# Four VectorE steps over 4096 columns, the load of b ahead, and a new order of all steps, in a gated recurrence with a rational feed-forward on one core

## The chip, the cores and the metric

The program runs on one core of one Trainium2 chip. The metric is the device time in microseconds of that core. Before the change the median of three runs is 218.05 us (217.76 to 218.08).

A core has five engines, each with its own queue of instructions that it works off in order: TensorE (matmuls; PE in the profile, its weight loads PEld), VectorE (DVE), ScalarE (ACT), GpSimd (POOL) and SyncE (SP, which here only issues transfers). Engines wait for each other through semaphores. Transfers are issued by an engine and then run by themselves.

## The reference

Two parts, the second fed by the first. The first is a recurrence with a gate per channel over 4 batches, 8 heads, 768 positions and a head size of 48. The second is a feed-forward layer over the 3072 tokens, 384 to 2048 to 384, with a quotient of two polynomials between its two products.

```python
f = 1.0 / (1.0 + np.exp(-f_logit))
for t in range(S):
    state = f[:, :, t, :, None] * state + np.einsum('bhd,bhe->bhde', k[:, :, t], v[:, :, t])
    y[:, :, t] = np.einsum('bhd,bhde->bhe', q[:, :, t], state)
...
h = x @ w_in
h2 = h * h
h3 = h2 * h
P = a[0] + a[1] * h + a[2] * h2 + a[3] * h3
Q = 1.0 + np.abs(b[0]) * np.abs(h) + np.abs(b[1]) * h2
g = P / (Q + 1e-06)
return (g @ w_out).astype(np.float32)
```

## The kernel before, in words

The work is cut into 12 units: a unit is one batch and 256 positions (3 stretches of positions, 4 batches). Within a unit the recurrence is done for two chunks of 128 tokens with matmuls, and the layer then takes the unit's 256 tokens as the columns of 16 blocks of 128 rows of the 2048, so a whole unit of the layer is a tile of 128 x 4096 and a quarter of it (four blocks) is 128 x 1024.

The steps of a unit, by the names that the order uses, with the lines of their functions:

- loads: `ld` of f, k, q on SP's queue and of v on POOL's (L200); the weights `wi` and `wo` in four pieces each on POOL's queue (L206, L212); the small `a` and `b` by `ab_` (L219), on SP's or ACT's queue.
- gate: `ef` and `ls` (ACT, L278 and L283) make log decay; `cs` sums it along positions (PE, L293); `A` takes its exponentials (ACT, L309); `xa` multiplies q and k by them (DVE, L315).
- attention: `T` turns q and k (PE, L327), `Te` takes that out of PSUM (L337 on ACT, L339 on DVE), `sc` multiplies q and k (PE, L352), `mk` masks (DVE, L360), `vm` copies a part of v (POOL, L367), `yb` and `yi` build the output (PE, L374), `kv` and `si` the next state (PE, L421 and L432), `ae` and `st` scale it (ACT L445, DVE L449), `ye` takes the output out of PSUM, scaled, as xT (ACT, L439).
- layer: `h` multiplies by w_in, four blocks to a call (PE, L458); `hy` takes the result out of PSUM as bf16 (ACT, L488); `sq` squares (DVE, L492; `sa` does the same on ACT from PSUM, L496); `ab` clears the sign bits (DVE, L500); the denominator's sum z + h2 is made by `u` on PE (L508), by `zv` on DVE (L518) or by `zd`, an accumulating DMA that POOL issues (L522); `ln` or `lz` (ACT, L513, L526) and `ex` (ACT, L530) make the reciprocal as exp(-log); `p1`, `p2`, `pm` (DVE, L534, L539, L548) and `tv` (DVE, L556) or `ta` (an accumulating DMA from POOL, L552) build the numerator in `gall`; `gm` multiplies by the reciprocal (DVE, L560); `o` multiplies by w_out, four blocks to a call and 128 tokens at a time (PE, L570); `oe` takes that out of PSUM (L577) and `so` stores it (L583).
- `cz`, `cu`, `ci`, `cm` fill constants, `fa`, `fb`, `fr` turn a and b into factors, `dz` issues matmuls whose result nobody reads (L302).

The order is written out by hand: one string, `ORDER`, lists every step, and each engine's queue is the steps of that engine in the order of the string. The numbers behind a step's name are the unit, then the range of blocks or head pairs; `@n` names one of four PSUM slots of 4 KB a partition, each of which is free again when what was in it has been taken out; a last letter names the engine (`s` ACT, `v` DVE, `a` ACT's queue); `>name` holds a load back until the named step is done. The semaphores follow from the tiles: a step waits for whoever wrote what it reads and for whoever still reads what it overwrites. Tiles have few buffers: `hy` and `gall` (the key `g`) three of 128 x 4096, `h2` and `z` two, `lq` and `qi` one, the loaded f, k, q, v three each.

```python
    def p1(n, m0, m1):
        s = unit(n)
        return nc.vector.tensor_scalar(fl(big(s, "g", "gall", 3), m0, m1), fl(s["hy"], m0, m1),
```

In the order before, VectorE's `sq`, `ab`, `pm` and `gm` take a unit in halves (2048 columns) or quarters, while `p1` and `p2` of units 1 to 10 already take 4096.

Of the kernel before, what the change touches and what calls it, by code (L numbers as in the profile page):

```python
# [113 lines left out]
def kernel(  # L114
# [371 lines left out]
    def hy(n, m0, m1):  # L486
        s = unit(n)
        nc.scalar.copy(fl(big(s, "hy", "hy", 3), m0, m1), fl(s["hp", m0], 0, m1 - m0))  # L488
# [140 lines left out]
```

## Time and profile before

| what | value |
|---|---|
| median of 3 runs | 218.05 us (217.76, 218.05, 218.08) |
| span of the profiled execution, first to last instruction | 216.3 us |
| TensorE busy | 203.2 us, 3166 matmuls |
| VectorE busy | 202.7 us, 246 instructions |
| ScalarE busy | 200.8 us, 211 instructions |
| GpSimd busy | 81.6 us, 91 instructions |
| granted TensorE clock | 1.000 |
| moved by DMA | 42.13 MB |

How to read it: the profile is one execution, with a start and a length for every instruction. A row of the timeline has the start in microseconds, the length, the engine, the line of the kernel, the operation, `out<-in` with the shapes, and how many instructions the row merges; in square brackets stands how long the engine was idle before it and who ended that. A row of the groups has the count, then busy time in microseconds and the mean of one in nanoseconds, then idle time before the group's instructions. Lengths overlap: an instruction's row starts a little before the row ahead of it has ended, so the time that one instruction costs in a full queue is the distance from its start to the next start.

### The profile page before, as it was taken

The page shows a single profiled execution, that of the slowest core. Times are in us where ns is not written, and L with a number is a line of the kernel's source. Part 1 is how long each engine was busy: PE and PEld are TensorE (multiplying, and loading weights), DVE is VectorE, ACT ScalarE, POOL GpSimd, SP SyncE. Part 2 cuts the span into 40 slices and gives each one's busy share as a digit, 9 for nine tenths or more (in the row PEclk, how much of TensorE's full clock was granted, in tenths as well). Part 3 has the DMA queues.
Part 4 walks back from the last instruction along what each step waited for, and adds up shares of the span by engine and source line. Part 5 has one row for each costly group of instructions (what it writes and reads, how often), then busy time and mean ns, then how long its engine had stood idle before and what let it go on. Part 6 is the DMA issues. An engine that isn't in the chain of part 4 may idle for free.

```text
span 216.3 us, 7159 instructions
## 1 busy us (share of the span) xinstructions
PE 203.2 (94%) x3166; PEld 140.1 (65%) x3166; DVE 202.7 (94%) x246; ACT 200.8 (93%) x211; POOL 81.6 (38%) x91
## 2 busy tenths in 40 slices
PE   6989989699799999999999999999999999999993
PEld 2457658468377657658758658668668678676551
DVE  3588999999999999999999999999999999999991
ACT  4746899999999999999999999999999999999991
POOL 5250247120157803014954205954232516433300
PEclk9999999999999999999999999999999999999999
DMA  5999999999598999958999997999889793999863
GB/s 132 248 226 194 243 212 226 207 221 250 136 246 143 231 237 271 149 101 195 197 232 216 211 251 179 173 234 222 160 159 228 142 162 70 170 194 188 154 234 145
DMA packets 60910, 42.13 MB, mean 195 GB/s; under 512 B 51152, under 2 KB 54992, under 8 KB 60880
## 3 DMA queue, kind: packets, MB, share of 16 engines
q0 software_dynamic: 21232, 22.81, 66.0%
q1 hardware_dynamic: 39360, 18.68, 33.7%
q8 instruction: 24, 0.39, 0.7%
q10 hardware_dynamic: 288, 0.20, 0.3%
q14 instruction: 6, 0.05, 0.1%
HBM read 25.17 MB, written 4.72 MB: 138 GB/s over the span
## 4 chain that ended last, share of the span: by engine, by line
ACT 42%; DVE 21%; PE 18%; DMA 8%; issue 6%; POOL 3%; POOLq 0%; ACTq 0%; DVEq 0%
ACT qi L530 11%; ACT hy L488 10%; PE op L570 9%; ACT lq L526 8%; DMA fn<-in_f_logit_dram 4%; DMA z<-h 4%; PE warm L302 3%; DVE gall L548 3%; ACT A L309 3%; DVE scm L360 3%; DVE qkp L315 3%; PE hp L458 2%; DVE gall L560 2%; DVE gall L556 2%; ACT qkT L337 2%
## 5 line engine op out<-in xcount | busy, mean ns | idle before, releaser
L570 PE MATMUL op<-w_out_sb,gall 128*128 128x384 bf16 x384 | 70.1, 326 | 0.4 <-ACT hy L488 0.4
L458 PE MATMUL hp<-xT,w_in_sb 128*128 128x256 bf16 x564 | 65.3, 272 | 1.3 <-ACT xT L439 1.1
L458 PEld LDWEIGHTS <-w_in_sb 128*128 128x128 bf16 x564 | 55.0, 98 | 11.0 <-issue 2.8
L570 PEld LDWEIGHTS <-gall 128*128 128x128 bf16 x384 | 35.5, 98 | 23.6 <-DVE gall L560 0.9
L488 ACT CAST hy<-hp 128x1024 bf16<-128x1024 f32 x48 | 47.4, 1073 | 1.7 <-PE hp L482 1.2
L530 ACT ACTIVATE qi<-lq 128x2048 bf16<-128x2048 f32 (+1 forms) x26 | 46.9, 1845 | 0.0
L367 POOL COPY vmp<-vn 128x128 bf16<-128x128 bf16 x24 | 33.7, 1417 | 32.1 <-DMA vn<-in_v_dram 18.9
L526 ACT ACTIVATE lq<-z 128x2048 f32<-128x2048 bf16 (+1 forms) x20 | 36.9, 1846 | 0.6 <-DMA z<-h 0.5
L552 POOL DMA_DIRECT2D gall<-hy x17 | 14.8, 926 | 50.7 <-ACT A L309 11.5
L522 POOL DMA_DIRECT2D z<-h x18 | 17.3, 1065 | 36.3 <-issue 10.5
L560 DVE TENSOR_TENSOR gall<-gall,qi 128x2048 bf16<-128x2048 bf16 (+1 forms) x26 | 29.6, 1143 | 0.3 <-ACT qi L530 0.2
L548 DVE TENSOR_TENSOR gall<-gall,h 128x2048 bf16<-128x2048 bf16 (+1 forms) x26 | 29.4, 1138 | 0.0
L492 DVE TENSOR_TENSOR h<-hy 128x2048 bf16<-128x2048 bf16 (+1 forms) x26 | 27.3, 1059 | 1.5 <-ACT hy L488 1.4
L360 DVE TENSOR_TENSOR scm<-sc,mask 128x1024 bf16<-128x1024 f32 x24 | 28.4, 1211 | 0.0
L309 ACT ACTIVATE A<-cs 128x768 f32<-128x768 f32 (+1 forms) x26 | 19.6, 816 | 0.0
L500 DVE TENSOR_SCALAR z<-hy 128x2048 uint16<-128x2048 uint16 (+1 forms) x28 | 17.1, 618 | 0.1
L534 DVE TENSOR_SCALAR gall<-hy,a_sb 128x4096 bf16<-128x4096 bf16 (+1 forms) x14 | 16.9, 1210 | 0.2 <-ACT hy L488 0.2
L539 DVE TENSOR_SCALAR hy<-hy,a_sb 128x4096 bf16<-128x4096 bf16 (+1 forms) x14 | 16.6, 1184 | 0.0
L200 POOL DMA_DIRECT2D vn<-in_v_dram x12 | 13.2, 1104 | 2.2 <-PE y L374 2.2
L315 DVE TENSOR_TENSOR qkp<-kn,A 128x768 bf16<-128x768 f32 (+1 forms) x13 | 11.5, 887 | 2.0 <-ACT A L309 2.0
L278 ACT ACTIVATE fn<-fn 128x768 f32<-128x768 f32 (+1 forms) x13 | 10.7, 825 | 2.8 <-DMA fn<-in_f_logit_dram 2.7
L337 ACT COPY qkT<-tp 128x1024 f32<-128x1024 f32 (+1 forms) x12 | 12.5, 1041 | 0.7 <-PE tp L327 0.7
(72 smaller groups left out, 262.2 us busy)
## 6 DMA issues: line engine op xcount, KB each, us to landing
gall<-hy POOLq DMA_DIRECT2D x16, 512.0 KB, 6.7
z<-h POOLq DMA_DIRECT2D x15, 512.0 KB, 7.4
fn<-in_f_logit_dram SPq DMA_DIRECT2D x11, 384.0 KB, 7.4
kn<-in_k_dram SPq DMA_DIRECT2D x11, 384.0 KB, 9.8
qn<-in_q_dram SPq DMA_DIRECT2D x11, 384.0 KB, 7.2
out_dram<-osb SPq DMA_DIRECT2D x11, 384.0 KB, 4.1
vn<-in_v_dram POOLq DMA_DIRECT2D x12, 192.0 KB, 8.0
w_in_sb<-in_moe_w_in_dram POOLq DMA_DIRECT2D x4, 384.0 KB, 8.2
```

What stands on the lines that cost most here:

```text
L309: nc.scalar.activation(t, src, AF.Exp, scale=1.0 if x else -1.0)
L315: return nc.vector.tensor_mul(s["qk"][:, :, x, hh, 0:D], s["qk"[x]][:, hh].rearrange("p h i d -> p i h d"), A_sb[:, :, x].rearrange("p i ( ...
L360: return nc.vector.tensor_mul(t, s["sc", g].rearrange("s r a i t -> s (r a) (i t)"), mb)
L367: nc.gpsimd.tensor_copy(s["vm"][:, :, :, 32 * x:32 * x + 16], src)
L458: nc.tensor.matmul(t[:, m - m0, :], w_in_sb[:, kk, m * P:(m + 1) * P], s["x"][:, kk].rearrange("p i j t -> p (i j t)"), start=(kk == 0), s ...
L488: nc.scalar.copy(fl(big(s, "hy", "hy", 3), m0, m1), fl(s["hp", m0], 0, m1 - m0))
L492: return nc.vector.tensor_mul(fl(big(s, "h2", "h2", 2), m0, m1), fl(s["hy"], m0, m1), fl(s["hy"], m0, m1))
L526: nc.scalar.activation(fl(lq, m0, m1), fl(s["z"], m0, m1), AF.Ln, scale=regs[2], bias=1.0 + 1e-6)
L530: nc.scalar.activation(fl(qi, m0, m1), fl(lq, m0, m1), AF.Exp, scale=-1.0)
L548: return nc.vector.tensor_mul(fl(s["g"], m0, m1), fl(s["g"], m0, m1), fl(s["h2"], m0, m1))
L560: return nc.vector.tensor_mul(fl(s["g"], m0, m1), fl(s["g"], m0, m1), fl(qi, m0, m1))
L570: nc.tensor.matmul(s["op", j][:, j, 0:DM], s["g"][:, m, P * j:P * j + P], w_out_sb[:, m, :], start=(s["on", j] == 1), stop=(s["on", j] == KF))
```

## The change

The order string is written anew: 861 steps become 823. What it does differently, as counts over the whole program:

| step | before | after |
|---|---|---|
| `sq` on DVE | 18 halves, 8 quarters | 9 whole, 2 halves, 8 quarters |
| `sa` on ACT | 4 quarters | none |
| `ab` | 20 halves, 8 quarters | 9 whole, 2 halves, 8 quarters |
| `pm`, `gm`, each | 22 halves, 4 quarters | 9 whole, 4 halves, 4 quarters |
| `tv` on DVE | 6 halves, 3 quarters | 4 halves, 1 quarter |
| `ta` by DMA | 16 halves, 1 quarter | 18 halves, 3 quarters |
| `zv` on DVE | 2 halves | 1 half, 1 quarter |
| `zd` by DMA | 15 halves, 3 quarters | 16 halves, 2 quarters |
| `hy` | 48 on ACT | 47 on ACT, 1 on DVE |
| `ye` | all on ACT | unit 8 and the first piece of unit 0 on DVE |
| `oe` | last unit's first half on DVE | that and unit 10 on DVE |

The whole ones, 4096 columns at once, are those of units 2 to 10. All other steps, the matmuls among them, are the same in number and shape, and stand in another order: `a` is loaded ahead of f on SP's queue; unit 2's f is held back behind `mk 0 1` as before, but `mk 0 1` now comes ahead of `mk 0 0`; the last of the w_in pieces is issued behind unit 1's v and `vm` steps.

The first and the last lines of the string and some between (those that are left out change as well), and the functions:

```diff
 ORDER = """
-ld 0 f 2 4; cz 0; ab_ b a; cu 0; cz 1; ld 0 f 0 2; ld 1 f; ci; cu 1; ld 0 v; ld 0 k 0 2; ld 0 k 2 4; fa
-ld 0 q 2 4; ef 0 2 4; ls 0 2 4; cm; ef 0 0 2; dz 9 @2; cs 0 2 4 @2; fr; cz 3; ls 0 0 2; ld 0 q 0 2; ab_ a s
-ld 1 k; dz 5 @3; cs 0 0 2 @3; ef 1; ld 1 q; ls 1; vm 0 1; A 0 1 0 2; wi 12 16 >ls.1; dz 4 @0; cs 1 @0
-A 0 1 2 4; xa 0 1 0 2; A 0 0 2 4; wi 8 12; cz 2; A 0 0 0 2; xa 0 1 2 4; dz 3 @1; kv 0 @2; wi 4 8
-xa 0 0 0 2; si 0 0; ae 0; dz 1 @1; T 0 0 2 @1; wi 0 4; xa 0 0 2 4; st 0 0; Te 0 0 2 s; T 0 2 4 @3; A 1 1
...
-ex 3 8 16; o 2 1 12 16; st 5 0; zd 4 0 8; o 2 0 12 16; mk 5 1; o 2 0 4 8; ex 3 0 8; p1 4 0 16; yi 5 1 @3
...
-tv 11 8 12; o 11 1 0 4; gm 11 8 12; o 11 0 0 4; ex 11 12 16; tv 11 12 16; o 11 0 8 12; gm 11 12 16
-oe 10 0 2 s; so 10 0 2 s; o 11 1 8 12; o 11 0 12 16; oe 11 0 1 v; so 11 0 1 s; o 11 1 12 16; oe 11 1 2 s
-so 11 1 2 a
+cu 0; ab_ a s; ab_ b a; cz 3; ld 0 f 2 4; ld 0 f 0 2; cz 0; cu 1; dz 9 @0; ld 1 f; cz 1; ld 0 q 2 4; ci; cz 2
+ld 0 k 2 4; cm; ld 0 k 0 2; ld 0 v; ld 0 q 0 2; fa; ld 1 k; ld 1 q; ef 0 0 2; dz 4 @1; ef 0 2 4; fr; ls 0 2 4
+ef 1; cs 0 2 4 @0; ls 0 0 2; A 0 0 2 4; cs 0 0 2 @2; A 0 1 2 4; dz 5 @1; xa 0 0 2 4; A 0 0 0 2; ls 1; vm 0 1
+wi 8 12; xa 0 1 2 4; A 0 1 0 2; wi 12 16 >ls.1; T 0 2 4 @0; xa 0 1 0 2; wi 4 8; Te 0 2 4; kv 0 @3; vm 0 0
+xa 0 0 0 2; sc 0 1 @1; ld 1 v; T 0 0 2 @2; mk 0 1; si 0 0; Te 0 0 2 s; ae 0; ld 2 f >mk.0.1; sc 0 0 @2; st 0 0
...
+ld 3 k; vm 1 0; kv 1 @0; ld 4 f; A 2 1; vm 1 1; ab 0 12 16; ld 3 q; wi 0 4; si 1 0; ae 1; A 2 0; ld 4 q
...
+yb 5 2 4; o 1 0 4 8; ld 8 v; ye 5 s; st 5 1; ld 9 q; T 6 @2; p1 4 0 16; oe 1 0 2 s; cs 7 @0; Te 6 s; so 1 0 2 s
...
+gm 11 12 16; ex 11 0 4; o 11 0 8 12 @3; tv 11 0 4; ex 11 4 8; o 11 0 12 16; gm 11 0 4; o 11 1 12 16; oe 9 0 2 s
+gm 11 4 8; o 11 0 0 4; oe 10 0 2 v; so 9 0 2 s; o 11 0 4 8; o 11 1 0 4; so 10 0 2 s; oe 11 0 1 v; o 11 1 4 8
+so 11 0 1 s; oe 11 1 2 s; so 11 1 2 a
 """
...
     def ye(n, *args):
-        k0, k1 = [x for x in args if x != "s"] or (0, KD)
+        k0, k1 = [x for x in args if x not in ("s", "v")] or (0, KD)
         s = unit(n)
         if "x" not in s:
             s["x"] = at.tile([P, KD, 2, UB, R], BF16, name="xT", bufs=2)
-        return nc.scalar.mul(s["x"][:, k0:k1].rearrange("p k i j t -> p j (k i) t"),
-                             s["y"][:, :, k0 * C:k1 * C].rearrange("p j (k t) -> p j k t", t=R), regs[0])
+        dst = s["x"][:, k0:k1].rearrange("p k i j t -> p j (k i) t")
+        src = s["y"][:, :, k0 * C:k1 * C].rearrange("p j (k t) -> p j k t", t=R)
+        if "v" in args:
+            return nc.vector.tensor_scalar(dst, src, sig[:, 0:1], None, op0=ALU.mult)
+        return nc.scalar.mul(dst, src, regs[0])
...
-    def hy(n, m0, m1):
-        s = unit(n)
-        nc.scalar.copy(fl(big(s, "hy", "hy", 3), m0, m1), fl(s["hp", m0], 0, m1 - m0))
+    def hy(n, m0, m1, eng="s"):
+        s = unit(n)
+        (nc.scalar.copy if eng == "s" else nc.vector.tensor_copy)(
+            fl(big(s, "hy", "hy", 3), m0, m1), fl(s["hp", m0], 0, m1 - m0))
```

143 lines of the change are left out of this document (67 added, 76 removed).

## The prediction

> **What bounds the kernel now.** I read the page first, then the busy time by stage, then the instruction groups by shape, then the timeline of the start and of the end.
>
> ```profile
> PE 203.2 (94%) x3166; PEld 140.1 (65%) x3166; DVE 202.7 (94%) x246; ACT 200.8 (93%) x211; POOL 81.6 (38%) x91
> ...
> 0.00:10.00 10.00, 8.02 (x31) 3.31 (x32) 4.49 (x28) 6.35 (x11) 3.85 (x15) 1.00 0.94 185
> 10.00:20.00 10.00, 9.19 (x206) 6.34 (x204) 8.10 (x14) 4.50 (x9) 3.90 (x6) 1.00 1.24 216
> ...
> 30.00:210.00 180.00, 173.88 (x2730) 122.86 (x2731) 178.95 (x190) 178.93 (x180) 71.65 (x67) 1.00 1.01 195
> ```
>
> The columns are stage, length, then PE, PEld, DVE, ACT, POOL, granted clock, DMA share, GB/s. From 30 to 210 us VectorE is busy 178.95 of 180 and ScalarE 178.93. TensorE shows 173.88, but a matmul's row overlaps the next, so that figure flatters it. No queue is the single bound; VectorE is idle for 1.05 us in those 180, so what it saves or gains there moves the end nearly one to one. Its other idle time, 13.6 less 1.05, lies in the start and in the end:
>
> ```profile
> 190.54 5.40 PE L458 MATMUL hp<-xT,w_in_sb 128*128 128x256 bf16 x48 [0.17 <-ACT xT L439]
> 201.26 11.53 PE L570 MATMUL op<-w_out_sb,gall 128*128 128x384 bf16 x68
> ...
> 210.57 0.69 DVE L560 TENSOR_TENSOR gall<-gall,qi 128x1024 bf16<-128x1024 bf16 x1 [0.15 <-ACT qi L530]
> ...
> 212.83 0.48 ACT L577 COPY osb<-op 128x384 f32<-128x384 f32 x1 [1.60 <-PE op L570]
> ```
>
> The last product (`gm`, L560) ends at 211.26, TensorE's last matmul at 212.79: 1.53 later. What follows (copy, store) takes until 216.3. The median of the runs, 218.05, is 1.75 above this span; I work on the span and add 1.75.
>
> **The change, part by part.** *VectorE's wide steps.* Rows that stand together give the time from one instruction's start to the next, since a single row overlaps its successor.
>
> ```profile
> 38.49 2.34 DVE L492 TENSOR_TENSOR h<-hy 128x2048 bf16<-128x2048 bf16 x2
> 40.76 0.68 DVE L500 TENSOR_SCALAR z<-hy 128x2048 uint16<-128x2048 uint16 x1
> 41.36 0.54 DVE L449 TENSOR_TENSOR state<-sv,alast 128x384 bf16<-128x384 f32 x1
> ...
> 54.50 1.21 DVE L492 TENSOR_TENSOR h<-hy 128x2048 bf16<-128x2048 bf16 x1
> ...
> 195.94 0.68 DVE L492 TENSOR_TENSOR h<-hy 128x1024 bf16<-128x1024 bf16 x1
> 196.54 0.75 DVE L500 TENSOR_SCALAR z<-hy 128x1024 uint16<-128x1024 uint16 x2
> 197.21 1.28 DVE L492 TENSOR_TENSOR h<-hy 128x1024 bf16<-128x1024 bf16 x2
> 198.41 0.42 DVE L500 TENSOR_SCALAR z<-hy 128x1024 uint16<-128x1024 uint16 x1
> ```
>
> A product of 2048 columns costs 2.34 − 1.21 = 1.13; of 1024, 1.28 − 0.68 = 0.60. So 1024 more columns cost 0.53, and 4096 cost 1.13 + 2 × 0.53 = 2.19: a merged pair saves 0.07. The mask step `ab` costs 0.60 (40.76 to 41.36) and 0.75 − 0.42 = 0.33, hence 1.14 for 4096, and saves 0.06. No row has a product of 4096; the price could lie from 2.19 − 0.1 to 2.26 (no gain), and I take the straight line. With the counts of the two order strings:
> - `sq`: 18 of 2048 and 8 of 1024 (25.14) become 9 of 4096, 2 of 2048 and 8 of 1024 (26.77): +1.63, because four blocks that ScalarE squared (`sa`) now come here.
> - `ab`: 20 and 8 (14.64) become 9, 2 and 8 (14.10): −0.54.
> - `pm` and `gm`: 22 and 4 (27.26) become 9, 4 and 4 (26.63): −0.63 each.
> - `tv`: 6 and 3 (8.58) become 4 and 1 (5.12): −3.46; these sums go to accumulating DMAs. `zv`: one of two shrinks to 1024: −0.53.
>
> For the merge, the Trainium skill ("VectorE: DVE Perf Modes", "Side-by-side: where the cycles go for N=2048 bf16") charges each instruction a start of about 150 cycles at 0.96 GHz, an estimate of 0.16 us a merge, and by it the 36 merges would save 5.6 us where the rows give 2.5, and the time would be 3.1 lower than the sum below. The single rows (1.21, 0.68) agree with that charge, but the steps between starts show that more than half of it overlaps the instruction before; so it gets no chance of its own.
>
> *Steps that come to VectorE* (the first piece of unit 0's `ye`, unit 8's `ye`, one `hy`, one `oe`):
>
> ```profile
> L360 DVE TENSOR_TENSOR scm<-sc,mask 128x1024 bf16<-128x1024 f32 x24 | 28.4, 1211 | 0.0
> L577 DVE COPY osb<-op 128x384 f32<-128x384 f32 x1 | 0.6, 558 | 0.9 <-PE op L570 0.9
> L439 ACT ACTIVATE xT<-y 128x768 bf16<-128x768 f32 x11 | 9.6, 871 | 0.0
> L577 ACT COPY osb<-op 128x768 f32<-128x768 f32 x11 | 9.4, 854 | 0.0
> L488 ACT CAST hy<-hp 128x1024 bf16<-128x1024 f32 x48 | 47.4, 1073 | 1.7 <-PE hp L482 1.2 <-PE hp L458 0.5
> ```
>
> VectorE has no such cast or scaling here. `hy` (1024 from PSUM) is nearest to L360's 1.21, less an overlap of 0.08: 1.13. The 768-wide `ye` and `oe` lie between L577's 0.56 for 384 and L360: 0.9 each; the 256-wide piece 0.4. Together 3.3, between 2.2 (half rate as for bf16) and 4.0. VectorE's sum: 1.63 − 0.54 − 1.26 − 3.46 − 0.53 + 3.3 = −0.86, bounds −2.0 to 0 with the merge's.
>
> *ScalarE* loses four `sa`, one `hy`, two `oe`/`ye` rows of 768 and a piece: 5 × 0.91 + 0.7 + 0.7 + 0.4 = 6.35 us (rows less 0.16 of overlap; a square of 1024 from PSUM is taken as L488's cast). Alone this is worth nothing, since VectorE and TensorE keep their work; it can only take away waits for ScalarE, which in 30 to 210 are within VectorE's 1.05.
>
> *TensorE* keeps 3166 matmuls, warm ones included: 0.
>
> *DMA.* Three more accumulations of 512 KB and one of 256 KB, 1.75 MB in all. They land 6.7 us after issue, beside work of other units; uncovered, each would hold a `gm` or `lz` for that long, which is a bound and not expected.
>
> ```profile
> gall<-hy POOLq DMA_DIRECT2D x16, 512.0 KB, 6.7
> ```
>
> *The start.*
>
> ```profile
> 5.91 0.63 SPq L219 DMA_DIRECT2D a_sb<-in_moe_a_dram  x1
> ...
> 9.02 0.56 DVE L315 TENSOR_TENSOR qkp<-kn,A 128x384 bf16<-128x384 f32 x1 [1.98 <-ACT A L309]
> 9.67 3.04 POOL L206 DMA_DIRECT2D w_in_sb<-in_moe_w_in_dram  x4
> ...
> 16.06 0.37 SPq L200 DMA_DIRECT2D fn<-in_f_logit_dram  x1
> ...
> 25.22 0.84 ACT L278 ACTIVATE fn<-fn 128x768 f32<-128x768 f32 x1 [0.41 <-DMA fn<-in_f_logit_dram]
> 25.74 0.53 POOL L367 COPY vmp<-vn 128x128 bf16<-128x128 bf16 x2 [11.84 <-DMA vn<-in_v_dram]
> ```
>
> `a` now goes ahead of the first f on SP's queue: +0.63 for everything behind f. Against it, f, q, k come in the order of use, and the load of unit 2's f is released by the first mask step, not the second (one mask step, 1.13, earlier; it had landed 9.1 after issue, holding ScalarE 0.41). VectorE keeps its small set-up work, done in the shadow of these loads. I take 0, bounds −0.5 and +1.
>
> *The end.* `oe 10` (0.9) now stands behind the last `gm` on VectorE, so that step comes 0.86 + 0.9 = 1.76 earlier. Behind the `gm` before it TensorE has four groups of four matmuls (11.53 / 68 = 0.17 each, 2.7); these start 0.6 before the last `gm` ends, so 2.1 remain against 1.53: +0.55. Sum: 0 − 1.76 + 0.55 = −1.2; span 215.1, time **216.9**, own range 215.7 to 217.6.
>
> **The rivals.**
> 1. *The ring of `gall` (slower).* `gall` has three buffers, so `p1` of a unit waits for the last `o` of three units before. Adding the steps above along each queue (and 0.66 for four `o`; 5.40 / 4 less the last one's tail, 1.31, for twelve `h` matmuls) from a common start, `p1 4` began 10.7 us after `o 1` ended, `p1 7` 10.3, `p1 10` 12.5. Now it is −0.8, 1.2 and 0.7. `gm` of a whole unit also gives `o` nothing until all of it is done. If TensorE runs only a microsecond behind its own sum, VectorE waits at L534 in most units, with all its queue behind it. At 0.35 us in eight units it costs 2.8, against the −1.2: **219.6**. It decides from a total wait of 1.2, where the gain is gone. For it: TensorE's zero slack. Against: leads of 3 us at units 5, 6 and 9, and waits add up only if both engines drift apart.
> 2. *The first quarter of w_in comes late (slower).* All four pieces were issued by 12.71; now `wi 0 4` stands on POOL's queue behind two `vm` steps that wait for unit 1's v, which landed at 25.7. One piece of four less goes ahead of it (1.34 MB with v, where 1.73 took 16.1 us from 9.67), so v is there near 22; two `vm` and the issue take 1.3 more. Landing 5.7 to 10.6 later, the piece is there at 29 to 34; by the sum of its queue TensorE wants it near 31, with `h 1`, `cs 3` and `T 2` behind. A wait of 2.5, passed on to VectorE at the next `hy`, gives 218.05 − 1.2 + 2.5 = **219.3**.
>
> ```profile
> DMA to landing us min/median/max: 5.7/8.2/10.6
> ```
>
> 3. *No change.* TensorE's queue is as long as before and sets the end by itself: **218.0**.
> 4. *More.* With ScalarE 6.3 us lighter, h, Te and A come early, and VectorE's waits in the middle go too: −1.2, the 1.05 there, and 0.6 of the start's waits for A: **215.2**.
> 5. *POOL held off (slower).* Longer VectorE steps delay its copies:
>
> ```profile
> L367 POOL COPY vmp<-vn x24: 291/680/5656, 9.3 to 181.4; 128x128 bf16<-128x128 bf16 x24
> ```
>
> From 0.29 to 5.66 us for one shape: what stretches them is work beside them. Two of 24 a microsecond later where something waits for them: −1.2 + 2, **218.9**. The Trainium skill ("SBUF — State Buffer", "Who interferes with whom") has a lock between the two engines held for a whole instruction, so doubled steps would hold POOL twice as long; the spread agrees with it.
>
> **How the numbers follow.** Forecast 0.38, rival 4 0.12; rival 3 0.13; rivals 1, 2, 5 0.17, 0.15, 0.05. About 0.2% (0.44 us) is what a measurement can tell from no change. Faster 0.50, same 0.13, slower 0.37. Likeliest 216.9; the range reaches from rival 4 less the merge's bound, 214.8, to beyond rivals 1 and 2, 220.4.
>
> **What would show it.** Right: L492, L548 and L560 at 4096 with 2.2 between starts; VectorE busy near 202; the last L560 before 210; ScalarE idle and waiting for TensorE. Wrong: waits of VectorE's L534 row on TensorE summing above 1.2 (rival 1); a TensorE wait on w_in's DMA near 31 us (rival 2); TensorE without waits yet ending at 212.8 (rival 3); VectorE's moved steps above 4.0, or a merged pair that saves nothing.

## The result and the profile after

| | before | after |
|---|---|---|
| median of 4 runs each, same chip | 218.06 us (217.76 to 218.11) | 220.83 us (220.53 to 221.94) |
| ratio after / before | | 1.0116 (95% 1.008 to 1.0152) |
| span of the profiled execution | 216.3 us | 218.9 us (its time 220.61) |
| mean granted TensorE clock in it | 1.000 | 0.991 |

The change makes the kernel slower by 1.2%; 216.9 was forecast, and the measured time lies above the range too. The time less the span is 1.7 us, as before, so the question is where 2.6 us of span come from. First the page's busy row of the kernel after, then its busy time by stage (columns as in the prediction: stage, length, PE, PEld, DVE, ACT, POOL, granted clock, DMA share, GB/s):

```profile
PE 202.7 (93%) x3157; PEld 141.2 (65%) x3166; DVE 202.5 (93%) x212; ACT 194.9 (89%) x203; POOL 78.8 (36%) x95
```

```profile
0.00:10.00 10.00, 6.13 (x21) 2.51 (x22) 3.86 (x26) 4.33 (x8) 3.73 (x15) 1.00 0.83 155
10.00:20.00 10.00, 8.44 (x184) 5.24 (x182) 7.45 (x11) 4.69 (x10) 3.10 (x5) 0.83 1.23 227
...
30.00:210.00 180.00, 175.70 (x2734) 125.22 (x2741) 179.48 (x158) 176.96 (x176) 68.95 (x71) 1.00 1.05 203
```

From 30 to 210 us VectorE is busy for 179.48 (178.95 before): it waits no more there than before, and ScalarE has got its slack (176.96 after 178.93). A busy time does not show whether steps take longer than their price; that comes below. The first 20 us are worse: VectorE 3.86 + 7.45 against 4.49 + 8.10, ScalarE's first stage 4.33 against 6.35. In the second stage the granted clock is 0.83; the trace's record of it has one stretch of 3.41 us, from 10.06 to 13.47, at half speed.

The steps themselves, in the groups by line and shape of the kernel after (count, then busy us and mean ns, then idle before):

```profile
L544 DVE TENSOR_TENSOR gall<-gall,h 128x4096 bf16<-128x4096 bf16 x9 | 20.7, 2300 | 0.0
L488 DVE TENSOR_TENSOR h<-hy 128x4096 bf16<-128x4096 bf16 x9 | 20.5, 2280 | 0.1
L556 DVE TENSOR_TENSOR gall<-gall,qi 128x4096 bf16<-128x4096 bf16 x9 | 20.5, 2280 | 0.2 <-ACT qi L526 0.2
L530 DVE TENSOR_SCALAR gall<-hy,a_sb 128x4096 bf16<-128x4096 bf16 x10 | 13.7, 1368 | 0.0
L496 DVE TENSOR_SCALAR z<-hy 128x4096 uint16<-128x4096 uint16 x9 | 10.9, 1216 | 0.0
...
L483 DVE CAST hy<-hp 128x1024 bf16<-128x1024 f32 x1 | 1.2, 1218 | 0.0
L434 DVE TENSOR_SCALAR xT<-y,sig 128x768 bf16<-128x768 f32 x1 | 1.0, 1009 | 0.0
L573 DVE COPY osb<-op 128x768 f32<-128x768 f32 x1 | 0.9, 949 | 0.0
```

A product of 4096 takes 2.28 and, from start to start, 2.20; the steps that came to VectorE take 1.22, 1.01 and 0.95. Nothing waits at L530 (idle 0.0), and the wide products wait for 0.3 in all.

**A ledger.** For every VectorE step I take its real start less the sum of the step prices ahead of it (from start to start, as in the prediction), which I call VectorE's lag: it grows only by waits and stretched steps. At 30 us it is −0.2 before and 2.2 after, at 45 us 0.2 and 3.65, at the start of the last `gm` 3.5 (start 210.57) and 5.6 (start 211.01). Then the difference of 2.6 in the span is: start, up to 45 us, +3.4; from there to the last `gm`, 1.95 of new lag against 3.3, −1.35; the sum of the step prices −1.6; from the start of the last `gm` to the end 7.9 against 5.7, +2.2.

*The start.* The timeline of the kernel after, with before's first gate step under it (the rest of before's start is in the prediction):

```profile
0.81 0.38 SPq L211 DMA_DIRECT2D a_sb<-in_moe_a_dram  x1
...
1.25 1.52 SPq L192 DMA_DIRECT2D fn<-in_f_logit_dram  x3
...
6.84 0.94 ACT L270 ACTIVATE fn<-fn 128x384 f32<-128x384 f32 x2 [4.75 <-DMA fn<-in_f_logit_dram]
...
10.23 0.56 DVE L307 TENSOR_TENSOR qkp<-qn,A 128x384 bf16<-128x384 f32 x1 [3.38 <-DMA qn<-in_q_dram]
```

```profile
4.42 0.52 ACT L278 ACTIVATE fn<-fn 128x384 f32<-128x384 f32 x1 [2.33 <-DMA fn<-in_f_logit_dram]
```

ScalarE's first step is 2.42 us later, though part of that is that it now takes the second piece of f first and both pieces in a row. What moved meanwhile is in the transfer view of the first 12 us, in slices of 0.3 us, after and then before:

```profile
GB/s 0 0 0 0 0 0 2 2 1 2 1 71 114 98 141 222 289 316 305 320 303 229 213 207 199 237 236 241 267 267 266 260 265 264 255 262 264 264 259 232
```

```profile
GB/s 0 0 0 0 0 0 70 135 121 102 174 139 196 264 270 282 301 324 318 282 241 202 178 184 188 192 202 222 243 313 324 312 289 279 242 253 259 261 266 256
```

From 1.8 to 3.3 us the kernel after moves 1 to 2 GB/s where the one before already moved 70 to 174: `a` is 2 KB written in 16-byte pieces to 128 partitions, and f stands behind it on the queue. The Trainium skill ("DMA: Bandwidth & Descriptors", "Queues, rings and completion order") says that each DMA engine works off a queue's descriptors in ring order, and the rows agree: f, issued 0.44 behind `a`, brings the rate up only from 3.3 us on.

Between 20 and 30 us the waits are these:

```profile
24.06 0.84 ACT L270 ACTIVATE fn<-fn 128x768 f32<-128x768 f32 x1 [0.85 <-DMA fn<-in_f_logit_dram]
...
26.71 0.43 DVE L496 TENSOR_SCALAR z<-hy 128x1024 uint16<-128x1024 uint16 x1 [0.40 <-ACT hy L483]
...
27.72 0.56 DVE L444 TENSOR_TENSOR state<-sv,alast 128x384 bf16<-128x384 f32 x1 [0.58 <-ACT alast L440]
```

From 30 to 45 us VectorE waits for nothing, in either kernel (busy for 15.00 of 15.00). The lag still grows by 1.45 in the kernel after and by 0.4 before, so there it is steps that take longer than their price (VectorE's rows, then GpSimd's):

```profile
35.31 1.94 DVE L496 TENSOR_SCALAR z<-hy 128x2048 uint16<-128x2048 uint16 x3
37.17 0.76 DVE L488 TENSOR_TENSOR h<-hy 128x1024 bf16<-128x1024 bf16 x1
...
35.45 2.90 POOL L204 DMA_DIRECT2D w_out_sb<-in_moe_w_out_dram  x3
37.75 3.43 POOL L359 COPY vmp<-vn 128x128 bf16<-128x128 bf16 x3
```

The three steps at 35.31 (`ab` of 2048 and twice of 1024) cost 1.86 up to the next start, where their prices make 1.26. Beside them GpSimd issues three quarters of w_out in a row and then copies; before, it issues these one by one between 31.05 and 38.88. Of the 2.4 us of stretch that the whole trace of the kernel after has from 30 us on, 2.2 lie in steps beside which GpSimd works. No run moves these issues alone, so that they are the cause is likely and not shown.

*The end*, in the timeline of the kernel after (rows of several engines):

```profile
206.64 7.31 PE L566 MATMUL op<-w_out_sb,gall 128*128 128x384 bf16 x44
...
210.22 1.48 DVE L556 TENSOR_TENSOR gall<-gall,qi 128x1024 bf16<-128x1024 bf16 x2
...
211.56 3.06 SPq L579 DMA_DIRECT2D out_dram<-osb  x3
...
213.99 0.48 ACT L573 COPY osb<-op 128x384 f32<-128x384 f32 x1 [2.46 <-PE op L566]
...
214.50 0.35 ACTq L579 DMA_DIRECT2D out_dram<-osb  x1
```

The last `gm` ends at 211.70, TensorE at 213.95, 2.25 later (1.53 before). From there to the end of the span it takes 4.95 (3.5 before), because the stores of units 9 and 10 now leave in the same 3 us as those of the last unit.

### The profile page after: what moved, and what is told of

The parts are those of the page before. It is cut to its first block, busy times and chain, and to the rows that moved or that the text cites. A ratio compares the mean times of both kernels' runs of the same rounds, so it can differ in the third digit from the quotient of the medians.

```text
span 218.9 us, 7125 instructions
## 1 busy us (share of the span) xinstructions
PE 202.7 (93%) x3157; PEld 141.2 (65%) x3166; DVE 202.5 (93%) x212; ACT 194.9 (89%) x203; POOL 78.8 (36%) x95
## 4 chain that ended last, share of the span: by engine, by line
ACT 37%; PE 30%; DVE 17%; DMA 7%; issue 6%; SPq 1%; ACTq 0%; DVEq 0%
PE op L566 14%; ACT qi L526 9%; ACT hy L483 9%; ACT lq L522 7%; DMA fn<-in_f_logit_dram 7%; PE hp L453 6%; ACT A L301 3%; DVE h L488 3%; DVE scm L352 3%; DVE gall L530 3%; PE y L366 2%; ACT osb L573 2%; ACT lsp L275 2%; DVE z L496 2%; PE u L504 2%
## 5 line engine op out<-in xcount | busy, mean ns | idle before, releaser
L453 PE MATMUL hp<-xT,w_in_sb 128*128 128x256 bf16 x564 | 66.4, 272 | 1.4 <-ACT xT L435 0.6
L483 ACT CAST hy<-hp 128x1024 bf16<-128x1024 f32 x47 | 48.9, 1105 | 0.7 <-PE hp L453 0.7
L548 POOL DMA_DIRECT2D gall<-hy x21 | 21.4, 1086 | 46.5 <-ACT hy L483 11.9
L359 POOL COPY vmp<-vn 128x128 bf16<-128x128 bf16 x24 | 25.4, 1166 | 28.7 <-DMA vn<-in_v_dram 22.3
L488 DVE TENSOR_TENSOR h<-hy 128x4096 bf16<-128x4096 bf16 (+2 forms) x19 | 28.5, 1506 | 0.1
L556 DVE TENSOR_TENSOR gall<-gall,qi 128x4096 bf16<-128x4096 bf16 (+2 forms) x17 | 28.2, 1660 | 0.4 <-ACT qi L526 0.2
L544 DVE TENSOR_TENSOR gall<-gall,h 128x4096 bf16<-128x4096 bf16 (+2 forms) x17 | 28.3, 1668 | 0.0
L192 POOL DMA_DIRECT2D vn<-in_v_dram x12 | 17.3, 1445 | 21.0 <-DVE gall L552 9.5
L530 DVE TENSOR_SCALAR gall<-hy,a_sb 128x4096 bf16<-128x4096 bf16 (+1 forms) x14 | 17.1, 1221 | 0.0
L496 DVE TENSOR_SCALAR z<-hy 128x4096 uint16<-128x4096 uint16 (+2 forms) x19 | 16.5, 875 | 0.4 <-ACT hy L483 0.4
L307 DVE TENSOR_TENSOR qkp<-qn,A 128x768 bf16<-128x768 f32 (+1 forms) x13 | 11.6, 893 | 3.4 <-DMA qn<-in_q_dram 3.4
```

The costliest lines, as they stand in the source:

```text
L359: nc.gpsimd.tensor_copy(s["vm"][:, :, :, 32 * x:32 * x + 16], src)
L453: nc.tensor.matmul(t[:, m - m0, :], w_in_sb[:, kk, m * P:(m + 1) * P], s["x"][:, kk].rearrange("p i j t -> p (i j t)"), start=(kk == 0), s ...
L483: (nc.scalar.copy if eng == "s" else nc.vector.tensor_copy)(fl(big(s, "hy", "hy", 3), m0, m1), fl(s["hp", m0], 0, m1 - m0))
L488: return nc.vector.tensor_mul(fl(big(s, "h2", "h2", 2), m0, m1), fl(s["hy"], m0, m1), fl(s["hy"], m0, m1))
L544: return nc.vector.tensor_mul(fl(s["g"], m0, m1), fl(s["g"], m0, m1), fl(s["h2"], m0, m1))
L556: return nc.vector.tensor_mul(fl(s["g"], m0, m1), fl(s["g"], m0, m1), fl(qi, m0, m1))
```

## The experiments

Times vary between chips and runs (before: 217.4 to 219.9 in all), so ratios are against runs of before on the same chip. Lag and last `gm` (start, in us) are those of the profiled execution; its clock stands beside its span. These rows are of one execution each, and loads land a little differently from one to the next: e13's first `h`, with the same order up to there as e8, waits 1.35 for w_in at 17.7 us, where e8's waits for no load. All kernels compute the whole result.

| run | ratio (95%) | span, clock | lag at 20 / 30 / 45 | last `gm` |
|---|---|---|---|---|
| before | 1 | 216.3, 1.000 | −0.9 / −0.2 / 0.2 | 210.57 |
| after | 1.0116 (1.008 to 1.0152) | 218.9, 0.991 | 0.8 / 2.2 / 3.65 | 211.01 |
| e1_a_late | 1.0081 (1.005 to 1.0112) | 218.3, 0.990 | −1.35 / 0.6 / 2.4 | 210.76 |
| e2_before_a_first | 1.0105 (1.0047 to 1.0163) | 218.2, 1.000 | 1.3 / 2.3 / 2.3 | 212.53 |
| e3_warm | 1.0073 (1.0048 to 1.0099) | 219.8, 0.991 | 0.8 / 2.6 / 4.1 | 213.30 |
| e4_split | 1.0137 (1.0102 to 1.0172) | 220.3, 0.989 | 0.0 / 2.0 / 3.5 | 213.78 |
| e5_tail | 1.0063 (1.0044 to 1.0082) | 218.7, 0.992 | 0.0 / 2.0 / 3.5 | 212.14 |
| e6_act | 1.0089 (1.0051 to 1.0128) | 219.2, 0.984 | −1.9 / 4.3 / 5.8 | 212.67 |
| e7_merge_before | 1.0175 (1.013 to 1.022) | 220.0, 0.997 | −0.6 / 0.15 / 1.4 | 214.29 |
| e8_all | 1.0065 (1.0033 to 1.0098) | 218.4, 0.991 | 0.0 / 2.5 / 6.2 | 212.03 |
| e9_cut78 | 1.0181 (1.0142 to 1.022) | 220.4, 0.984 | 0.1 / 4.75 / 7.0 | 214.08 |
| e10_cut134 | 1.0657 (1.0613 to 1.07) | 230.2, 0.962 | −1.3 / 0.0 / 4.8 | 223.86 |
| e11_cut180 | 1.0655 (1.0613 to 1.0698) | 230.2, 0.963 | −0.9 / 0.4 / 0.8 | 223.84 |
| e12_cut219 | 1.0275 (1.0224 to 1.0326) | 221.6, 0.998 | −1.1 / 0.1 / 0.1 | 215.21 |
| e13_hy_first | 1.0145 (1.006 to 1.0229) | 219.9, 0.992 | −1.8 / 2.5 / 6.4 | 213.53 |
| e14_win_first | 1.0105 (1.0044 to 1.0166) | 218.0, 0.997 | 0.0 / 3.0 / 4.5 | 211.21 |
| e15_pm_gm | 1.0044 (1.0014 to 1.0074) | 217.4, 0.999 | −1.25 / −0.1 / −0.1 | 211.68 |
| e16_v_first | 1.0007 (0.9979 to 1.0035) | 216.4, 1.000 | 0.1 / 2.0 / 3.5 | 210.04 |
| e17_v_first_hy | 1.0139 (1.0094 to 1.0184) | 219.6, 0.992 | 0.05 / 4.3 / 6.85 | 213.20 |
| e18_ef5 | 1.0031 (0.9998 to 1.0064) | 215.9, 1.000 | 0.1 / 1.9 / 3.4 | 209.56 |

**The load of `a`, in both orders.**

```diff
 e1_a_late (the changed order)
-cu 0; ab_ a s; ab_ b a; cz 3; ld 0 f 2 4
+cu 0; ab_ b a; cz 3; ld 0 f 2 4
...
-ld 0 q 0 2; fa; ld 1 k
+ld 0 q 0 2; ab_ a s; fa; ld 1 k
 e2_before_a_first (the order before)
-ld 0 f 2 4; cz 0; ab_ b a
+ab_ a s; ld 0 f 2 4; cz 0; ab_ b a
```

> The changed kernel with one step moved back: the load of a behind the last load of unit 0's q on SP's queue, where it stood before. Theory A (the small load of a ahead of f holds the queue): the first ef starts at 4.4 to 5.0 us instead of 6.84, VectorE waits for q under 1.5 us instead of 3.4, the granted clock is 1.000 again; time 216.8 to 218.3, some 2.5 to 4 below the changed kernel's 220.83. Theory O (the new order of loads and steps at the start is slower by itself): ef gains only the 0.4 us that issuing a takes, time 220.0 to 220.5. Theory C (the halved clock alone costs the time): ef earlier by 2, but the pause of TensorE stays, the clock stays below 1, time above 219.5.

> The kernel before with one step moved: the load of a ahead of the first f on SP's queue. Theory A: the first ef comes 1.7 to 2.5 us later than 4.42, time 218.06 + 1.5 to 2.6 = 219.6 to 220.7. Theory O: only the issue of 0.4 to 0.6 us is added, time 218.2 to 218.7. Theory C: a loss above 1 only if the granted clock falls below 1.

The one edit in the order before costs 1.9 us of span and the whole of it shows in VectorE's lag at 30 us (2.3 for −0.2). Its first gate step, in e2's timeline, comes 1.63 us later than the same step before:

```profile
6.05 0.52 ACT L278 ACTIVATE fn<-fn 128x384 f32<-128x384 f32 x1 [3.96 <-DMA fn<-in_f_logit_dram]
```

Taking `a` out of the way in the changed order gives VectorE 2.15 us by 20 us; 1.6 are left at 30, 1.25 at 45 and 0.25 at the last `gm`. From 20 to 30 us the rows of e1 say where they went: ScalarE stands before `ef 2` until f of unit 2 has landed, with `hy` of unit 0 queued behind it, and VectorE waits for that `hy`.

```profile
22.48 0.84 ACT L270 ACTIVATE fn<-fn 128x768 f32<-128x768 f32 x1 [1.56 <-DMA fn<-in_f_logit_dram]
...
25.13 0.43 DVE L496 TENSOR_SCALAR z<-hy 128x1024 uint16<-128x1024 uint16 x1 [1.11 <-ACT hy L483]
```

And the clock was halved again, at another place, from 43.46 to 46.87; between 45 and 50 us the lag grows by 1.0 (0.1 in the kernel after). So the first `ef` starts early (5.12 for 6.84), nearly as theory A had it, but the time, a median of 220.21, and the clock come out as A did not have them, and the time where theory O put it. e1's stages:

```profile
40.00:45.00 5.00, 3.28 (x75) 1.69 (x74) 4.75 (x7) 4.09 (x7) 2.20 (x2) 0.85 1.24 204
45.00:50.00 5.00, 5.00 (x97) 3.13 (x95) 4.10 (x6) 3.78 (x5) 1.33 (x2) 0.81 1.25 204
```

**The clock.** e3 gives TensorE nine more warming matmuls in its gaps near 8 us.

```diff
-ld 1 q; ef 0 0 2; dz 4 @1; ef 0 2 4
+ld 1 q; ef 0 0 2; dz 9 @1; ef 0 2 4
-A 0 0 2 4; cs 0 0 2 @2
+A 0 0 2 4; dz 4; cs 0 0 2 @2
```

> The changed kernel, a still ahead of f, with nine more warming matmuls between 7 and 10 us, so that TensorE has no long pause there. The granted clock should be 1.000. Theory C: time falls by 1.5 to 2.5, to 218.3 to 219.3. Theory A: the first product still waits for q until 10.2 us, so no more than 1 us comes back: 219.8 to 220.8.

The clock stays at 1.00 from 10 to 20 us, and VectorE's lag at 20 us is the same 0.8: the halved clock at 10 us had cost nothing, because the loads were later. In its place the clock falls from 45.3 to 48.7:

```profile
10.00:20.00 10.00, 7.80 (x191) 5.17 (x190) 7.49 (x12) 4.97 (x10) 3.50 (x6) 1.00 1.15 214
...
45.00:60.00 15.00, 14.57 (x283) 10.11 (x284) 13.84 (x16) 13.65 (x14) 1.40 (x2) 0.89 1.33 207
```

There it costs 1.3 us of lag (4.1 to 5.4 at 50 us); in the kernel after, without it at that place, the lag goes from 3.65 to 3.75. The clock is not all of the loss: in two of e3's five executions its mean is 0.999, and their spans are 217.9 and 218.3, still above the 216.0 to 217.3 of before on that chip. The median of 220.10 is where theory A put it, not theory C.

**What the wide steps are worth, in this order and in the old one.** e4 takes the 36 steps of 4096 as two of 2048 at the same place; e7 merges 26 pairs in the order before, each at its later half's place; e15 merges only the 16 of `pm` and `gm`.

```diff
 e4_split
-ab 2 0 16; ... sq 2 0 16
+ab 2 0 8; ab 2 8 16; ... sq 2 0 8; sq 2 8 16
 e7_merge_before, e15_pm_gm
-pm 5 8 16; ... pm 5 0 8
+... pm 5 0 16
```

> The changed kernel with each of the 36 steps over 4096 columns split into two of 2048 at the same place in the order. If a merged pair saves 0.07 us on a VectorE without pauses: +2.0 to +2.6, 222.8 to 223.5. If the wide steps cost something themselves (the first o waits for the whole gm, GpSimd is held off longer): no change or faster, at most 221.

> The kernel before in its own order, with 26 pairs of its halves of sq, ab, pm and gm of units 1 to 10 joined into one step over 4096 columns, at the place of the later half, wherever nothing between them needs the earlier one. If the join by itself pays 0.07 us each on a full VectorE: 26 x 0.07 = 1.8 lower, ratio 0.990 to 0.994. If the later start of the first half's work makes ScalarE or TensorE wait as much: ratio 0.996 to 1.010.

> The kernel before with 16 pairs of pm and gm alone taken as one step of 4096 at the place of the later half (sq and ab stay halves). Theory (e7's waits came from sq and ab, which need hy of the whole unit at once; pm and gm read what has long been written): 16 x 0.07 = 1.1 us of VectorE's work saved and no new wait over 0.3 us, span 215.2 to 216, ratio 0.993 to 0.999. Rival (a merged gm holds back the first half's output matmuls, and a merged pm the ta or ex behind it): TensorE or VectorE waits for them, span 216.5 to 218, ratio 1.001 to 1.008.

Splitting raises the sum of the prices by 2.48 (0.07 a pair, as priced). Against e5_tail, which has the same lag at 45 us and its clock halved at nearly the same place, the last `gm` starts 1.6 later: that is what merging is worth in the changed order, by these two executions. The medians do not confirm it: e4's is only 0.2% above the kernel after, within both intervals, where 2.0 to 2.6 us were expected. In the old order merging is a loss: e7 saves 1.8 of prices and adds 5.5 of lag, at steps like these, where a whole unit's `hy` has to be there at once (e7's timeline):

```profile
39.11 2.29 DVE L485 TENSOR_TENSOR h<-hy 128x4096 bf16<-128x4096 bf16 x1 [1.01 <-ACT hy L481]
...
121.68 1.23 DVE L493 TENSOR_SCALAR z<-hy 128x4096 uint16<-128x4096 uint16 x1 [1.69 <-ACT hy L481]
```

`pm` and `gm` alone read what has long been there, and still do not pay: 1.1 of prices saved, 2.2 of lag added. The largest new wait is at the state step of unit 10. In e15's timeline ScalarE has no idle time ahead of the factor for it, which is there at 164.93 (165.37 before), so VectorE cannot come sooner; the first half of `gm` that had filled its time in the order before (1.2 us, from 161.24) now stands behind this wait as part of the whole one, and TensorE waits for that in turn:

```profile
162.89 1.96 ACT L520 ACTIVATE lq<-z 128x2048 f32<-128x2048 bf16 x1
164.71 0.22 ACT L439 ACTIVATE alast<-sv 128x8 f32<-128x8 f32 x1
```

```profile
164.95 0.56 DVE L443 TENSOR_TENSOR state<-sv,alast 128x384 bf16<-128x384 f32 x1 [1.22 <-ACT alast L439]
165.43 2.28 DVE L554 TENSOR_TENSOR gall<-gall,qi 128x4096 bf16<-128x4096 bf16 x1
```

```profile
167.77 0.50 PE L564 MATMUL op<-w_out_sb,gall 128*128 128x384 bf16 x2 [1.44 <-DVE gall L554]
```

A merge at the later half's place thus takes away work that covered a wait for ScalarE, which is nearly as full as VectorE in the order before.

**The end and ScalarE's free time.** e5 takes units 9 and 10 out of PSUM and stores them some steps earlier, both on ScalarE; e6 is e1 with `hy 0 8 12` and the first piece of `ye 0` back on ScalarE; e8 is e6 with e5's end, `ef 0 0 2` behind `ls 0 2 4`, and the load of f of unit 2 released by `xa 0 1 0 2`.

```diff
 e5_tail
-ex 11 4 8; o 11 0 12 16; gm 11 0 4; o 11 1 12 16; oe 9 0 2 s
-gm 11 4 8; o 11 0 0 4; oe 10 0 2 v; so 9 0 2 s; o 11 0 4 8; o 11 1 0 4; so 10 0 2 s
+ex 11 8 12; oe 9 0 2 s; so 9 0 2 s; ... ex 11 4 8; oe 10 0 2 s; so 10 0 2 s; o 11 0 12 16
 e6_act
-hy 0 8 12 v; ... ye 0 0 1 v
+hy 0 8 12; ... ye 0 0 1 s
 e8_all
-ld 2 f >mk.0.1
+ld 2 f >xa.0.1.0.2
```

> The changed kernel with the copies out of PSUM of units 9 and 10 (oe) on ScalarE and earlier, so that their stores leave before the last 5 us. Theory T (the changed end is longer by 2.2 us than before, of which 1.4 are stores of units 9 and 10 that go out with the last unit's): last data lands 2.1 to 2.5 us after TensorE's last matmul instead of 3.5, time lower by 0.8 to 1.6, ratio to the kernel before 1.004 to 1.008. Rival (the longer end is TensorE's four groups alone, stores hidden): under 0.4 us lower, ratio above 1.009.

> As e1_a_late (a loaded late), and hy of unit 0's third quarter and the first piece of unit 0's ye on ScalarE again, as before the change. Theory S (in the first 25 us VectorE is short of time and ScalarE stands idle for 2.8 us, so these two steps were moved the wrong way): VectorE's own queue loses 1.5 us there, time 0.8 to 1.6 below e1_a_late, ratio to the kernel before 1.001 to 1.005. Rival (the start waits for loads and for TensorE, whoever takes the copies): within 0.4 us of e1_a_late, ratio 1.006 to 1.010.

> The changed kernel with all that the start and the end lost taken back: a late, both unit 0 steps on ScalarE, ef in the order of the loads, unit 2's f released by an earlier step, oe and so of units 9 and 10 early. If the three losses add (start 3.5, end 1.4, of 2.6 net) and the middle keeps its gain of 1.6: time 2 to 3.5 below the changed kernel, ratio to the kernel before 0.995 to 1.003. If a halved clock in some window is what costs the changed order, whatever its start: ratio above 1.005 and a mean clock of 0.99.

In e5 the span ends 3.7 us after TensorE, 1.25 less than after, so the stores were part of it; the halved clock at 45.7 us hides most of that in its profiled span, and its median gains 0.5%. e6 gains nothing: at 30 us its lag is 4.3, since VectorE now waits twice for 2.29 us for the `hy` of unit 0, at 20.1 and at 26.4. e8 puts the pieces together and is still 0.65% slower than before, with a clock of 0.991, as its clock rival had it, and with a new wait in it. The fourth quarter of w_in is issued behind POOL's copy that waits for v of unit 1:

```profile
24.93 0.72 POOL L359 COPY vmp<-vn 128x128 bf16<-128x128 bf16 x2 [11.58 <-DMA vn<-in_v_dram]
...
25.59 0.74 POOL L198 DMA_DIRECT2D w_in_sb<-in_moe_w_in_dram  x1
...
33.62 4.36 PE L453 MATMUL hp<-xT,w_in_sb 128*128 128x256 bf16 x24 [2.39 <-DMA w_in_sb<-in_moe_w_in_dram]
```

**Is it the start's order alone?** Four kernels take the first 78, 134, 180 or 219 steps from the order before and what is left in the changed order, with e5's end.

```diff
-ORDER of e5_tail
+ld 0 f 2 4; cz 0; ab_ b a; cu 0; ... st 0 1; dz 1 @3
+ld 2 q; xa 1 0; h 0 8 12 @1; hy 0 8 12 v; T 1 @2; ...
```

> Spliced order: the first 78 steps of the order before (up to the last piece of attention of unit 0, about 18 us; a behind b and the loads of unit 0, all four quarters of w_in ahead of v of unit 1), from there the changed order with each remaining step once, and the tail of e5_tail. Theory (the changed order loses its 3.5 us against the order before in the start, by the load of a ahead of f and by the fourth quarter of w_in and f of unit 2 that come late; from 50 us on it is 1.4 better, and the wide steps save 1.6): VectorE's lag at 20 us is -0.9 as before, but the changed order from 20 to 30 us asks for f, q, k of unit 2 ahead of their landing, so about half of the loss is met again: span 217 to 217.8, ratio 0.999 to 1.004. Rival (what is lost is the clock, halved for 3.4 us after pauses of TensorE, wherever they fall): clock 0.98 to 0.99 again and span 218 to 219, ratio 1.003 to 1.01.

> As the 78-step splice, but the first 134 steps (some 30 us, up to the state and the first two pieces of attention of unit 1) are those of the order before. Theory (loss sits ahead of 30 us): lag at 30 us -0.2 as before and no wait for f of unit 2; then the changed order's own gains: span 216.3 - 1.6 (wide steps) - up to 1.4 + up to 2.0 (end) = 215.3 to 216.7, ratio 0.994 to 1.001. Rival (the gain of 1.4 in the middle was only the lag of the start being made good, since attention stood ahead): span 217 to 218, ratio 1.002 to 1.006.

> As the 78-step splice, with the first 180 steps (some 40 us, up to the first sums of unit 3) from the order before. Theory (loss ahead of 30 us): no better than the 134-step splice, within 0.3 us of its span. Rival (part of the loss lies between 30 and 45 us, where the changed order's TensorE paused for 1.2 and 0.65 us and the clock fell afterwards): 0.5 to 1.5 us shorter than the 134-step splice.

> As the 78-step splice, with the first 219 steps (some 50 us, into unit 2's steps) from the order before. Theory (the changed order needs attention further ahead than the order before has it at 50 us; merging in the old order cost 3.8): VectorE waits for hy and sc in units 2 and 3, span 217 or more. Rival (any start without loss will do): span 215.3 to 216.5, ratio 0.994 to 1.0.

e9 and e10 miss what either theory said, e11 fits its own only because it fails just as e10 does, and e12's span of 221.6 is what its theory had (217 or more), though VectorE waits there for other steps. e9 has before's loads: f of unit 2 lands at 25.2, just as before. But ScalarE asks for it 3.54 us ahead of that, where before it came to that step 0.41 ahead (row at 25.22 in the prediction), and VectorE stands behind:

```profile
25.17 0.84 ACT L270 ACTIVATE fn<-fn 128x768 f32<-128x768 f32 x1 [3.54 <-DMA fn<-in_f_logit_dram]
...
27.82 0.62 DVE L496 TENSOR_SCALAR z<-hy 128x1024 uint16<-128x1024 uint16 x1 [2.89 <-ACT hy L483]
```

e12 has no lag at 45 us and loses the start's gain directly behind the cut, since the changed order's rest counts on attention of units 3 and 4 that is not done yet:

```profile
52.55 0.56 DVE L444 TENSOR_TENSOR state<-sv,alast 128x384 bf16<-128x384 f32 x1 [1.67 <-ACT alast L440]
...
58.60 0.96 DVE L307 TENSOR_TENSOR qkp<-qn,A 128x768 bf16<-128x768 f32 x1 [3.27 <-ACT A L301]
```

e10 and e11 only show that loads were left in a wrong order at the cut: VectorE waits 11.55 us for k in e10, and 11.56 us in e11 behind a ScalarE that stands before f. They say nothing on the two theories.

**Steps or loads.** e13 (from e8) puts on ScalarE `hy 0 12 16` ahead of `ef 2`, on TensorE `h 0 4 8` ahead of `cs 2`, and moves three VectorE steps; e14 adds the fourth quarter of w_in ahead of the waiting copy; e16 (from e8) and e17 (from e13) only issue the third quarter behind v of unit 1; e18 adds to e16 `ef 5` behind `hy 0 0 4`.

```diff
 e13_hy_first
-ef 2; sc 1 0 @3; sc 1 1 @0; hb 0 12 16; mk 1 1; ls 2; hy 0 12 16; cs 2 @2
+sc 1 0 @3; sc 1 1 @0; hb 0 12 16; mk 1 1; hy 0 12 16; h 0 4 8 @2; ef 2; ls 2; cs 2 @1
-ab 0 12 16; ld 3 q
+ab 0 12 16; sq 0 12 16; p1 0 8 16; ld 3 q
-p1 1 0 16; ln 0 4 8; si 2 0; u 0 8 12 @0; ae 2; ef 4; st 2 0
+ln 0 4 8; si 2 0; u 0 8 12 @0; ae 2; ef 4; st 2 0; p1 1 0 16
 e14_win_first (on e13)
+wi 0 4; vm 1 0
 e16_v_first (on e8), e17_v_first_hy (on e13)
-xa 0 1 0 2; wi 4 8; Te 0 2 4
+xa 0 1 0 2; Te 0 2 4
-ld 1 v; T 0 0 2 @2; mk 0 1; si 0 0
+ld 1 v; T 0 0 2 @2; mk 0 1; wi 4 8 >xa.0.1.0.2; si 0 0
 e18_ef5 (on e16)
-ef 5; h 1 4 8 @2; sq 1 8 16; ta 0 8 16; hy 0 0 4
+h 1 4 8 @2; sq 1 8 16; ta 0 8 16; hy 0 0 4; ef 5
```

> e8_all with five steps moved: on ScalarE hy 0 12 16 stands ahead of ef 2 and ls 2 (which wait for f of unit 2), on TensorE h 0 4 8 ahead of cs 2, on VectorE sq 0 12 16 and p1 0 8 16 ahead of st 1 0, and p1 1 0 16 behind st 2 0. Theory (the start's waits are ScalarE standing on the late load, with hy behind it): the wait of ab 0 12 16 (1.1 to 2.4 us in the kernels before) goes, VectorE's lag at 30 us falls by 1 to 2, span 216 to 217.3, ratio 0.996 to 1.002. Rival (the start is bound by the bytes that the changed order asks for, in whatever order it waits): another step waits as long, at h 0 0 4 for w_in or at st 1 0 for v, and the span stays at 217.5 to 219, ratio 1.004 to 1.01.

> e13_hy_first with the load of the fourth quarter of w_in issued ahead of POOL's step that waits for v of unit 1, as in the order before. Theory (TensorE's wait of 2.4 us for that quarter in e8_all was its late issue): no wait of h 0 0 4, f of unit 2 and v of unit 1 land up to 1.7 us later, span 0.5 to 1.5 under e13_hy_first. Rival (the bytes decide): what h 0 0 4 gains, st 1 0 and A 2 lose, span within 0.5 of e13_hy_first.

> e8_all with one load moved: the third quarter of w_in (393 KB) is issued behind v of unit 1 on POOL's queue, not ahead of it. Theory (the order of issue sets the waits): v of unit 1 lands 1.5 to 2 us earlier than the 24.9 of e8_all, POOL's copies and the fourth quarter of w_in go with it, TensorE's wait of 2.4 us for that quarter shrinks below 1; span 217 to 218, ratio 1.0 to 1.005. Rival (the bytes decide, the queues share what the memory gives): v lands earlier but the third or fourth quarter of w_in later by as much, TensorE waits 1.5 or more for w_in; span 218 to 219, ratio 1.004 to 1.01.

> e13_hy_first with the same move. Theory (order of issue): the wait of st 1 0 (1.6 us in e13_hy_first) goes below 0.5, span 1 to 2 us under e13_hy_first's 219.9. Rival (bytes): h 0 4 8, which there stands ahead of cs 2 on TensorE, waits for the third quarter instead, and span stays above 219.

> e16_v_first with one step moved: on ScalarE ef 5, which waited 2.36 us there for its load, stands behind hy 0 0 4, not ahead of it. Theory (an early step that waits for a load holds what is queued behind it): VectorE's wait at ab 0 0 4 (0.74) and the ones it passes on go, span 215.3 to 216, ratio 0.994 to 0.999. Rival (ScalarE's order is not what is late, hy 1 4 8 and A 3 take the wait over): span 216 to 217, ratio 0.999 to 1.003.

e13 goes to its rival, and its span of 219.9 lies even above that: the wait of `ab 0 12 16` is gone, and `st 1 0` waits 1.5 us for what comes from v. e14 loses TensorE's wait for w_in (1.66 us in e13), as its theory had it, and keeps the one of `st 1 0`. e16 moves one transfer of 384 KB and gives back 2.0 us of the profiled span and 0.6% of the ratio, nearly all that e8 was behind. A part of it is the clock, 1.000 for 0.991, and how large a part is open: the two of e8's ten executions with a clock of 1.000 have spans of 216.4 and 216.5, e16's own. Its rows against those of e8: v is there at 21.94, 3.0 us earlier, the fourth quarter of w_in goes out 3.2 earlier, f of unit 2 holds ScalarE 0.40 (1.81 in e8), and no matmul waits for w_in:

```profile
20.99 0.84 ACT L270 ACTIVATE fn<-fn 128x768 f32<-128x768 f32 x1 [0.40 <-DMA fn<-in_f_logit_dram]
...
21.94 0.53 POOL L359 COPY vmp<-vn 128x128 bf16<-128x128 bf16 x2 [8.81 <-DMA vn<-in_v_dram]
22.41 0.77 POOL L198 DMA_DIRECT2D w_in_sb<-in_moe_w_in_dram  x1
```

The same move in e17 meets an `h 0 4 8` that now stands early, wants just that third quarter, and holds the state behind it for 4.0 us of lag:

```profile
24.77 2.37 PE L453 MATMUL hp<-xT,w_in_sb 128*128 128x256 bf16 x12 [2.52 <-DMA w_in_sb<-in_moe_w_in_dram]
```

So loads and steps decide together: a load in time for one order is late for another. e18's profiled span is the shortest of all, 215.9, yet its median is no better than before: the two runs with a clock of 1.000 and 0.998 have spans of 215.9, seven with 0.991 or 0.992 have 215.9 to 218.2, the three others 218.6 to 219.6.

## Why the prediction was wrong, step by step

- *Wide steps:* right for the prices. 2.20 was measured for 2.19, 0.07 a merge by e4, and the last `gm` came 1.64 earlier by its prices, where 1.76 was forecast.
- *Steps that come to VectorE:* right. `hy` costs 1.25 from start to start (20.89 to 22.14), `ye` and `oe` are 1.01 and 0.95 long, for 1.13, 0.9 and 0.9.
- *ScalarE:* its busy time fell by 5.9 (6.35 forecast), and it was right that this alone is worth little. Between 45 us and the last `gm` 1.35 was gained. Only part of that is rival 4's waits: from 45 to 205 us VectorE is idle for 0.52, before for 0.94; the rest are steps that were stretched less.
- *TensorE, 0:* right for its matmuls, but "0" left out that its new pauses let the granted clock fall. In the profiled execution of the kernel after, that happened where it cost nothing; in e3, e4 and e5 it cost about 1.0 to 1.3. Two of the four executions of the kernel after, at 0.984 and 0.987, have a lower clock than the profiled one, and spans of 219.2 and 220.2.
- *DMA accumulations:* right, nothing waited for them.
- *The start, "0, bounds −0.5 and +1":* this is the step that failed, +2.4 by 30 us and +3.4 by 45. The load of `a` was priced by its issue, 0.63; on the queue it costs 1.6 us of the first f, and 1.9 to 2.0 us of span in the order before (e2). In the changed order 1.25 of the lag at 45 us is `a`'s (e1), and 2.2 are left without it. The new order asks for f of unit 2 and v of unit 1 earlier than they land (e1, e9), with `hy` of unit 0 behind them; the forecast only looked at when the load of f was released. And from 30 to 45 us 1.1 more goes to stretched steps than before, not to waits; the forecast priced every VectorE step the same wherever it stands.
- *The end, +0.55:* the groups behind the last `gm` cost 0.7 for the 0.55 forecast. The stores that leave together, 1.45, were in no term.

The terms that were off: start +3.4, stores +1.45, middle −1.35, and 0.3 in small ones; that makes +3.8 on the forecast of −1.2, the 2.6 that were measured.

Of the rivals, 1 did not happen (L530 waited 0.0). Rival 3 did not either: TensorE has waits at the start and ends at 213.95, not at 212.8, and the time rose. Rival 2 did not show in the kernel after; it showed in e8, 2.39 us on TensorE, when the start was 1.6 us ahead of the kernel after (lag at 16 us, −1.7 for −0.1), so it lay directly behind the loss that was there. Rival 5 did not happen as told: POOL's 24 copies took 25.4 us in all after the change and 33.7 before. Their median rose from 0.68 to 1.13 us, but with the wide steps split in the same order (e4) it is 1.16, so the width is not what does it. What shows is the other direction, VectorE's own steps stretched beside GpSimd.

Settled: the load of `a` ahead of f costs 1.9 us of span in the order before (e2), and some 1.3 of the longer end are the stores that leave together (e5). Not settled: what would mend the rest of the start. e16 is as fast as before, but its lag at 45 us is 3.5, as in the kernel after. It gets its 2.5 us of span over the kernel after in other ways: two steps less on VectorE (`hy` and a piece of `ye`, 1.65 by their prices, which gained nothing in e6), against 0.7 more of lag at the last `gm`, and an end that is 1.5 shorter. How much of each median is the clock is open as well; it falls at places that differ between runs of one kernel. No version here is faster than before by more than the measurement can tell.

## What to carry to other kernels

A reordering that saves work on the busiest engine must also be priced at its start: for every load, when it lands in the old order and when the new order asks for it, with what is queued behind the step that asks. A tiny load that writes many small pieces goes behind the first big ones, not ahead. Before merging two steps, look at what each half released: the larger step saves a little every time, and its input must be there as a whole.
